# Five PSUM banks as five tiles in a spectral mixer with a gated feed-forward

## Chip, core and metric

One core of a Trainium2 chip. The metric is the time of one execution on the device in microseconds (us): 3697.88, the median of three runs (3697.82 to 3701.17).

## What is computed

For 8 sequences of 3072 positions and 256 channels: a real Fourier transform along the sequence, a complex 256x256 weight with a bias and a soft threshold on each frequency, the transform back; then for each of the 24576 rows an RMS norm and a gated feed-forward of width 1536.

```python
X = np.fft.rfft(x, axis=1); Xr, Xi = X.real, X.imag
Yr = Xr @ w_r - Xi @ w_i + b_r
Yi = Xr @ w_i + Xi @ w_r + b_i
Yr = np.sign(Yr) * np.maximum(np.abs(Yr) - 0.01, 0.0)      # Yi likewise
x = np.fft.irfft(Yr + 1j * Yi, n=3072, axis=1).reshape(24576, 256)
xn = x / np.sqrt(np.mean(x * x, axis=-1, keepdims=True) + 1e-06) * rms_g
g, val = xn @ w_gate, xn @ w_val
out = g * (1.0 / (1.0 + np.exp(-g))) * val @ w_out
```

## The kernel before

**The feed-forward.** The rows are cut into 48 tiles of 512, six to a sequence. A tile is transposed so that the channels lie on the partitions. The width of 1536 is cut into 12 slices of 128; a tile and a slice make a *step* (`step`, L944), 576 in all. A step multiplies its slice of the gate and value weights with the tile (the way up), takes Silu of the gate times the value (`h`), splits the product in a rounded half and a rest (`hs`, L952 and L953), and multiplies these with the slice of `w_out` into `acc` (the way down, `down`, L958 to L960), which is stored after twelve steps. Each fp32 product is three fp32r matmuls (high by high, high by low, low by high): this is why matmuls come in triples.

**Two ways up.** In 10 of the 48 tiles a step is *straight* (`straight`, L892): two sums of six 512-column matmuls into a g bank and a v bank (L901), Silu (L912), product (L913). In the other 38 tiles, 456 steps, it is *mixed* (`products`, L915): seven products of 128x128 by 256 columns in place of eight, from seven combinations `x` of the tile's blocks (`combine`) and weight combinations that are loaded for each step as `tr`. Product `own(0)` goes into `top` and is copied by ACT into `low` (L933), so that further products add to it there; ACT saves the pair of `add_` and `low` as it stands in `pq` (L935), more products add to both; DVE adds `pq` to the pair (`y`, L938); the last products go in, and ACT takes Silu of the pair of `top` and `low` (L941); DVE multiplies by `y` (L942). `top` and `add_` are halves of the g bank, `low` half of the v bank. So the pairs that L935, L938 and L941 read lie in two banks.

**The banks.** [...] One tile `up` (L288) holds five of them, `[P, 10, 256]`: halves 0 to 5 are three g banks, 6 to 9 two v banks; class `Bank` (L356) hands them out in turn. `acc` and `f` (the spectral products `pf`, `pm`, `pb` and transposes) have tiles of their own.

**The spectral work.** While a sequence's 72 steps run, the next sequence is transformed (`spectrum`): butterflies over 24 slots on DVE, then twelve units, each a forward product on PE (`pf`, L530), split, weight product (`pm`, L588 to L599), threshold, product back (`pb`, L650 to L658); butterflies and the norm at the end. During the last sequence's steps there is none of it.

**The order.** Every instruction group is first recorded by `op` with a due time in steps (`at`), an engine or two to choose from, a cost in us and the tokens that it reads and writes. `Plan.ordered` gives out buffers in turn; `Plan.schedule` places the groups one after the other on the engine that is free first, PE by smallest due time among what is ready; `emit` writes the program in this order, and the tile framework adds the semaphore waits, tile by tile. The plan counts each bank by itself (`BANKS`, L136). Constants set the due times: `LATER` for the way down, `DECODE` for the decoding of weights in the first sequence, `FIRST` and `LATER_ON` for the three parts of the spectral work within 72 steps, to which `BACK` is added.

```python
up_banks = pu.tile([P, 10, 256], F32, name="up")                                 # L288
pair = lambda k: up_banks[:, gb.h + k:vb.h + 1:vb.h - gb.h - k]                   # L921
```

## Time and profile before

| what | value |
|---|---|
| median of three runs | 3697.88 us |
| the profiled execution | 3696.22 us, span 3694.5 us |
| PE busy, its weight loads busy | 3098.2 us, 2771.7 us |
| DVE busy, ACT busy | 2259.1 us, 1879.8 us |
| mean granted TensorE clock | 0.994 |
| DMA | 577.69 MB, mean 156 GB/s |

The span runs from the first to the last instruction of the profiled execution. PE is TensorE's matmuls (their ends are modelled), PEld its weight loads, which one sequencer issues in front of them; DVE is VectorE, ACT is ScalarE, SP and POOL issue the DMAs. In a row, "up<-xn,tr" is written tile and read tiles, "idle before" the engine's idle time just in front of the group's instructions, and the names behind the arrows are the instructions whose end released them.

### The profile page before, as it was taken

The numbers are of one execution on the slowest core, as the hardware profiler recorded it, in microseconds if no ns is written. First come the engines' busy times: TensorE is split into PE (matmuls) and PEld (weight loads), VectorE is DVE, ScalarE is ACT, GpSimd is POOL, SyncE is SP. The second block draws the span as 40 slices with busy tenths as digits, with TensorE's granted clock in tenths as the row PEclk, the third lists the DMA queues.
The fourth block names the chain that finished last, engine by engine and source line by source line (L and its number), as shares of the span: only waits on it lengthen the run. The fifth ranks groups of instructions, "written<-read, shape, count | busy, mean of one in ns | idle before, by whom it ended". The sixth has DMA issues, their size and how long they took to land.

```text
span 3694.5 us, 56853 instructions
## 1 busy us (share of the span) xinstructions
PE 3098.2 (84%) x22147; PEld 2771.7 (75%) x22147; DVE 2259.1 (61%) x3994; ACT 1879.8 (51%) x3823; POOL 90.1 (2%) x176
## 2 busy tenths in 40 slices
PE   7679888889878888798888888888888888877777
PEld 6557876788768887787777887778877888766666
DVE  7786667656756557565675656756667566633343
ACT  2444655556545555455554555545554555443443
POOL 0000000000000000000000000000000000000000
PEclk9999999999999999999999999999999999999999
DMA  5354553455435554455544555345553555334443
GB/s 178 110 177 166 191 186 114 160 167 187 158 123 176 173 171 142 135 185 168 170 138 152 180 163 185 121 154 177 174 173 117 167 167 168 128 115 139 146 136 115
DMA packets 247023, 577.69 MB, mean 156 GB/s; under 512 B 23393, under 2 KB 80098, under 8 KB 246754
## 3 DMA queue, kind: packets, MB, share of 16 engines
q1 hardware_dynamic: 222562, 485.97, 39.7%
q0 software_dynamic: 24192, 88.09, 8.0%
q8 instruction: 174, 2.85, 0.3%
q14 instruction: 95, 0.78, 0.1%
HBM read 534.65 MB, written 39.32 MB: 155 GB/s over the span
## 4 chain that ended last, share of the span: by engine, by line
PE 71%; ACT 15%; DVE 10%; issue 3%; DVEq 0%; DMA 0%; ACTq 0%; SPq 0%
PE up L927 37%; PE acc L960 13%; PE up L901 10%; DVE y L938 6%; ACT pq L935 5%; ACT h L941 5%; ACT up L933 3%; PE pm L592 3%; PE pf L530 2%; DVE h L913 1%; ACT h L912 1%; PE up L710 1%; PE pm L588 1%; PE pb L655 1%; PE pt L867 1%
## 5 line engine op out<-in xcount | busy, mean ns | idle before, releaser
L927 PE MATMUL up<-xn,tr 128*128 128x256 f32 x5472 | 985.3, 293 | 262.6 <-ACT pq L935 86.8
L927 PEld LDWEIGHTS up<-xn,tr 128*128 128x128 f32 x5472 | 753.3, 188 | 395.1 <-ACT pq L935 124.3
L960 PE MATMUL acc<-wo,hs 128*128 128x256 f32 x6912 | 962.0, 279 | 2.2 <-DVE wo L810 1.1
L927 PE MATMUL up<-xn,wb 128*128 128x256 f32 x4104 | 730.8, 290 | 201.6 <-ACT h L941 94.2
L960 PEld LDWEIGHTS acc<-wo,hs 128*128 128x128 f32 x6912 | 874.4, 189 | 7.2 <-DVE wo L810 1.9
L927 PEld LDWEIGHTS up<-xn,wb 128*128 128x128 f32 x4104 | 569.4, 189 | 276.6 <-ACT h L941 123.6
L942 DVE TENSOR_TENSOR h<-h,y 128x512 f32<-128x512 f32 x456 | 315.2, 691 | 510.3 <-ACT h L941 509.0
L938 DVE TENSOR_TENSOR y<-up,pq 128x512 f32<-128x512 f32 x456 | 315.2, 691 | 405.6 <-PE up L927 304.3
L941 ACT ACTIVATE h<-up 128x512 f32<-128x512 f32 x456 | 272.4, 597 | 446.8 <-PE up L927 427.9
L935 ACT ACTIVATE pq<-up 128x512 f32<-128x512 f32 x456 | 272.4, 597 | 445.1 <-PE up L927 316.3
L953 DVE TENSOR_TENSOR hs<-h,hs 128x512 fp32r<-128x512 f32 x576 | 393.0, 685 | 100.4 <-ACT hs L952 99.2
L952 ACT ACTIVATE hs<-h 128x512 fp32r<-128x512 f32 x576 | 360.3, 626 | 88.6 <-PE acc L960 33.7
L901 PE MATMUL up<-xn,wb 128*128 128x512 f32 x1080 | 317.0, 404 | 43.2 <-ACT h L912 25.6
L933 ACT ACTIVATE up<-up 128x256 f32<-128x256 f32 x456 | 168.0, 368 | 345.5 <-PE up L927 245.8
L901 PEld LDWEIGHTS up<-xn,wb 128*128 128x128 f32 x1080 | 196.9, 190 | 106.8 <-ACT h L912 40.4
L912 ACT ACTIVATE h<-up 128x512 f32<-128x512 f32 x120 | 71.5, 596 | 192.5 <-PE up L901 169.7
L503 POOL DMA_DIRECT2D tab<-in_tabs_dram x168 | 89.3, 532 | 3047.1 <-PE pf L530 1491.0
L913 DVE TENSOR_TENSOR h<-h,up 128x512 f32<-128x512 f32 x120 | 81.3, 685 | 130.5 <-PE up L901 79.3
L901 PE MATMUL up<-xn,tb 128*128 128x512 f32 x360 | 128.5, 411 | 33.2 <-DVE h L913 23.6
L530 PE MATMUL pf<-tab,as 128*128 128x256 f32 x1008 | 134.0, 277 | 0.0
L530 PEld LDWEIGHTS pf<-tab,as 128*128 128x128 f32 x1008 | 123.9, 188 | 0.2
L592 PE MATMUL pm<-wm,xs 128*128 128x256 f32 x924 | 120.8, 277 | 0.0
(157 smaller groups left out, 3101.3 us busy)
## 6 DMA issues: line engine op xcount, KB each, us to landing
tr<-dt SPq DMA_DIRECT2D x456, 512.0 KB, 3.4
wo<-do SPq DMA_DIRECT2D x564, 256.0 KB, 2.7
tab<-in_tabs_dram POOLq DMA_DIRECT2D x168, 512.0 KB, 3.9
out_dram<-o SPq DMA_DIRECT2D x32, 512.0 KB, 3.2
seq<-in_x_dram SPq DMA_DIRECT2D x28, 512.0 KB, 5.4
tb<-db SPq DMA_DIRECT2D x27, 512.0 KB, 3.6
seq<-in_x_dram SPq DMA_DIRECT2D x25, 256.0 KB, 5.7
unit<-in_units_dram SPq DMA_DIRECT2D x12, 512.0 KB, 4.4
```

What stands on the lines that cost most here:

```text
L530: PE.matmul(ps[:, h, :], lhsT=r()[:, lp, ri, h * P:(h + 1) * P], rhs=f[:, rp, ri, :], start=(k + ri == 0), stop=(k == 2 and ri == 1),)
L592: PE.matmul(pm()[:, k], lhsT=(xr, xi)[k](lp, h), rhs=wm[:, rp, h, 1 + k, :], start=False, stop=(n == 2 and h == 1), skip_group_check=True,)
L901: PE.matmul((g, v)[k].flat(), lhsT=w(k, lp, c), rhs=xn()[:, rp, 2 * c:2 * c + 2, :].rearrange("p a b -> p (a b)"), start=((lp, rp, c) == t ...
L927: PE.matmul(dst(), lhsT=w(lp), rhs=xn()[:, rp, x, :], start=start and k == 0, stop=k == 2, skip_group_check=True)
L933: op("A", act(256), lambda _: A.activation(low(), top(), AF.Copy), [g], vb.first)
L935: op("A", act(512), lambda _: A.activation(pq()[:, ::-1, :], pair(1), AF.Copy), [g, v], pq.first)
L938: op("V", dve(512), lambda _: V.tensor_tensor(y(), pair(1), pq(), ALU.add), [g, v, pq.tok], y.first)
L941: op("A", act(512), lambda _: A.activation(s().rearrange("p (a b) -> p a b", a=2), pair(0), AF.Silu), [g, v], s.first)
L942: op("V", dve(512), lambda _: V.tensor_tensor(s(), s(), y().rearrange("p a b -> p (a b)"), ALU.mult), [y.tok], [s.tok])
L952: op("A", act(512), lambda _: A.activation(h()[:, 0], s(), AF.Copy), [s.tok], h.first)
L953: add(512, lambda f: f(h()[:, 1], s(), f32(h()[:, 0]), ALU.subtract), [s.tok], [h.tok])
L960: PE.matmul(o()[:, c, :], lhsT=h()[:, lp, c * P:(c + 1) * P], rhs=wo_()[:, rp, :], start=(i == 0 and k == 0 and c % 2 == 0), stop=(i == NF ...
```

## The change

The tile `up` becomes two pools of tiles of one bank each: two g banks and three v banks. `products` is rewritten so that each instruction of ACT and DVE works within one bank: `own(0)` and `mix(0)` go into the g bank (`p1`, `p5_`); ACT copies `p1` into `left` in the v bank (L931), ACT or DVE copies `p5_` into SBUF as `p5` (L932, 256 columns); after one product ACT copies `left` into `right` in the same bank (L934); after two more DVE adds `p5` to both halves (`y`, L938); Silu is done in two halves of 256, one from each bank (L939, L941). The 21 matmuls of a mixed step stay (L925 in place of L927), and so does the rest of the program. In the plan, `LATER` goes from 4.2 to 4.4, and the offsets of decoding and of the spectral work shift.

```diff
--- before.py
+++ after.py
@@ -32,12 +32,12 @@
 ORDER = [0, 9, 6, 3, 8, 4, 10, 2, 1, 7, 5, 11]
 LAM = 0.01
 PLAIN_OF = (5,)
-LATER = 4.2
+LATER = 4.4
 AHEAD = 60
-DECODE = (-4.5, -3.7, 0.4)
-BACK = 4.5
-FIRST = (16, 27, 50, 69.0)
-LATER_ON = (-1.5, 9, 48, 68)
+DECODE = (-5.0, -4.7, 0.4)
+BACK = 2.5
+FIRST = (16, 24.0, 51.5, 75.0)
+LATER_ON = (-3.0, 9, 48, 66.5)
 PLAIN = 3
 
 
@@ -133,7 +133,7 @@
 
     LAG = {"S": 2.2, "G": 3.0}
     STAY = 0.4
-    BANKS = ("gb0", "gb1", "gb2", "vb0", "vb1", "acc0", "f0")
+    BANKS = ("gb0", "gb1", "vb0", "vb1", "vb2", "acc0", "f0")
 
     def __init__(self):
         self.ops = []
@@ -271,7 +271,8 @@
 
     cp, bp, w1, w2, w4 = sbuf("cp", 1), sbuf("bp", 2), sbuf("w1", 1), sbuf("w2", 2), sbuf("w4", 4)
     wp, cq, q4, q3, q1, q2, sp = sbuf("wp", 1), sbuf("cq", 1), sbuf("q4", 4), sbuf("q3", 3), sbuf("q1", 1), sbuf("q2", 2), sbuf("sp", 1)
-    pu = ctx.enter_context(tc.tile_pool(name="pu", bufs=1, space=bass.MemoryType.PSUM))
+    pu = ctx.enter_context(tc.tile_pool(name="pu", bufs=2, space=bass.MemoryType.PSUM))
+    pv = ctx.enter_context(tc.tile_pool(name="pv", bufs=3, space=bass.MemoryType.PSUM))
     pa = ctx.enter_context(tc.tile_pool(name="pa", bufs=1, space=bass.MemoryType.PSUM))
     pf = ctx.enter_context(tc.tile_pool(name="pf", bufs=1, space=bass.MemoryType.PSUM))
     dp = ctx.enter_context(tc.tile_pool(name="dp", bufs=1, space=bass.MemoryType.DRAM))
@@ -285,7 +286,6 @@
     wb = cq.tile([P, NF, 3, 2, P], F32R, name="wb")
     dw = [[dp.tile([P, 2, n], F32, name=f"d{c}{i}") for i in range(NF)] for c, n in (("t", 512), ("o", D), ("b", 512))]
     df = [dp.tile([P, 2, 2, 2 * P], F32, name=f"df{g}") for g in range(NF // 2)]
-    up_banks = pu.tile([P, 10, 256], F32, name="up")
     ident = sp.tile([P, P], F32, name="ident")
     bias = sp.tile([P, 2, D], F32, name="bias")
     bias0 = sp.tile([P, D], F32, name="bias0")
@@ -327,7 +327,7 @@
         "seq": (bp, 2), "F": (w1, 1), "t4": (w1, 1), "o": (w1, 1), "m": (w1, 1), "a": (w1, 1), "k": (w1, 1), "z": (w1, 1),
         "ss": (w1, 1), "xf": (w1, 1), "xn": (w2, 2), "h": (w2, 2), "wo": (w4, 4),
         "tr": (q4, 4), "hs": (q3, 3), "G": (q1, 1), "as": (q1, 1), "xs": (q1, 1), "t3": (q1, 1), "st": (q1, 1), "pq": (q1, 1),
-        "gb": (None, 3), "vb": (None, 2), "acc": (pa, 1), "f": (pf, 1),
+        "gb": (pu, 2), "vb": (pv, 3), "acc": (pa, 1), "f": (pf, 1),
     }
 
     class Room:
@@ -357,11 +357,11 @@
 
 
         def __init__(self, tag, name):
-            super().__init__(tag, (), name)
-            self.h = 2 * (self.k % self.n) + (0 if tag == "gb" else 6)
+            super().__init__(tag, (P, 2, 256), name)
 
         def __call__(self, k=None):
-            return up_banks[:, self.h:self.h + 2] if k is None else up_banks[:, self.h + k]
+            t = super().__call__()
+            return t if k is None else t[:, k]
 
         def flat(self):
             return self().rearrange("p a b -> p (a b)")
@@ -913,13 +913,11 @@
         op("V", dve(512), lambda _: V.tensor_tensor(s(), s(), v.flat(), ALU.mult), [v.tok], [s.tok])
 
     def products(n, xn, i, s, tr):
-        pq, y = Room("pq", (P, 2, 256), f"pq{n}"), Room("m", (P, 2, 256), f"y{n}")
+        p5, y = Room("pq", (P, 256), f"p5{n}"), Room("m", (P, 2, 256), f"y{n}")
         own = lambda b: (lambda lp: wb[:, i, b, lp, :])
         mix = lambda b: (lambda lp: tr()[:, lp, P * b:P * (b + 1)])
-        gb, vb = Bank("gb", f"g{n}"), Bank("vb", f"v{n}")
-        g, v = gb.tok, vb.tok
-        top, low, add_ = (lambda: gb(0)), (lambda: vb(0)), (lambda: gb(1))
-        pair = lambda k: up_banks[:, gb.h + k:vb.h + 1:vb.h - gb.h - k]
+        one, two = Bank("gb", f"g{n}"), Bank("vb", f"v{n}")
+        p1, p5_, left, right = (lambda: one(0)), (lambda: one(1)), (lambda: two(0)), (lambda: two(1))
 
         def up(dst, w, x, tok, start=False):
             def go(_):
@@ -928,18 +926,20 @@
 
             op("P", mms(3, 256), go, [xn.part(f"h{k}") for k in (0, 2, 4, 6)] + [f"wb.{i // 2}", tr.tok], tok)
 
-        up(top, own(0), 0, gb.first + [f"go{n}"], True)
-        up(add_, mix(0), 4, [g])
-        op("A", act(256), lambda _: A.activation(low(), top(), AF.Copy), [g], vb.first)
-        up(low, mix(1), 5, [v])
-        op("A", act(512), lambda _: A.activation(pq()[:, ::-1, :], pair(1), AF.Copy), [g, v], pq.first)
-        up(low, mix(2), 1, [v])
-        up(add_, own(2), 6, [g])
-        op("V", dve(512), lambda _: V.tensor_tensor(y(), pair(1), pq(), ALU.add), [g, v, pq.tok], y.first)
-        up(low, mix(3), 3, [v])
-        up(top, own(1), 2, [g])
-        op("A", act(512), lambda _: A.activation(s().rearrange("p (a b) -> p a b", a=2), pair(0), AF.Silu), [g, v], s.first)
-        op("V", dve(512), lambda _: V.tensor_tensor(s(), s(), y().rearrange("p a b -> p (a b)"), ALU.mult), [y.tok], [s.tok])
+        up(p1, own(0), 0, one.first + [f"go{n}"], True)
+        up(p5_, mix(0), 4, [one.tok])
+        op("A", act(256), lambda _: A.activation(left(), p1(), AF.Copy), [one.tok], two.first)
+        op("AV", {"A": act(256), "V": dve(256)}, lambda e: A.activation(p5(), p5_(), AF.Copy) if e == "A" else V.tensor_copy(p5(), p5_()), [one.tok], p5.first)
+        up(left, mix(1), 5, [two.tok])
+        op("A", act(256), lambda _: A.activation(right(), left(), AF.Copy), [], [two.tok])
+        up(right, mix(2), 1, [two.tok])
+        up(left, own(2), 6, [two.tok])
+        up(p1, own(1), 2, [one.tok])
+        op("V", dve(512), lambda _: V.tensor_tensor(y(), two(), p5().unsqueeze(1).to_broadcast([P, 2, 256]), ALU.add), [two.tok, p5.tok], y.first)
+        op("A", act(256), lambda _: A.activation(s()[:, :256], p1(), AF.Silu), [one.tok], s.first)
+        up(right, mix(3), 3, [two.tok])
+        op("A", act(256), lambda _: A.activation(s()[:, 256:], right(), AF.Silu), [two.tok], [s.part("b")])
+        op("V", dve(512), lambda _: V.tensor_tensor(s(), s(), y().rearrange("p a b -> p (a b)"), ALU.mult), [y.tok, s.part("b")], [s.tok])
 
     def step(n, xn, i, mixed):
         s, h = Room("h", (P, 512), f"h{n}"), Room("hs", (P, 2, 512), f"hs{n}", F32R)
```

**PE, two mixed steps in the middle of the run.** Before, steps 312 to 314 of PE: `tr312` marks products of step 312 with loaded weights, `wb` those with resident ones; the fourth row's `tr313` belongs to step 313.

```order
L927 MATMUL up_147<-xn26_20353,wb_104 128x256 [waits Activation_49]
L927 MATMUL up_147<-xn26_20353,wb_104 128x256 x2
L960 MATMUL acc300_19823<-wo309_20217,hs309_20291 128x256 x3
L927 MATMUL up_147<-xn26_20353,tr313_20256 128x256 x3
L927 MATMUL up_147<-xn26_20353,wb_104 128x256 x3
L927 MATMUL up_147<-xn26_20353,tr314_20326 128x256 [waits DMAHW4_49]
L927 MATMUL up_147<-xn26_20353,tr314_20326 128x256 x2
L592 MATMUL pm5_3_20451<-wm_103,xs5_3_20384 128x256 [waits DVE_49]
L592 MATMUL pm5_3_20451<-wm_103,xs5_3_20384 128x256 x11
L927 MATMUL up_147<-xn26_20353,tr312_20198 128x256 [waits Activation_49]
L927 MATMUL up_147<-xn26_20353,tr312_20198 128x256 x2
```

The first row adds `own(2)` to step 312's g bank and waits for ACT; the row before the last adds to step 312's v bank and waits for ACT; all go to one tile, `up_147`. Now the same engine in steps 313 to 315 of the changed program, where `g314` and `v314` are the banks of step 314:

```order
L960 MATMUL acc300_20931<-wo310_21453,hs310_21536 128x256 [waits DMAHW3_49]
L960 MATMUL acc300_20931<-wo310_21453,hs310_21536 128x256 x2
L925 MATMUL v314_21683<-xn26_21465,tr314_21498 128x256 [waits Activation_49]
L925 MATMUL v314_21683<-xn26_21465,tr314_21498 128x256 x2
L960 MATMUL acc300_20931<-wo310_21453,hs310_21536 128x256 x6
L925 MATMUL v313_21619<-xn26_21465,tr313_21429 128x256 [waits DVE_49]
L925 MATMUL v313_21619<-xn26_21465,tr313_21429 128x256 x2
L925 MATMUL v314_21683<-xn26_21465,tr314_21498 128x256 [waits Activation_49]
L925 MATMUL v314_21683<-xn26_21465,tr314_21498 128x256 x2
L925 MATMUL v314_21683<-xn26_21465,wb_107 128x256 x3
L925 MATMUL g314_21666<-xn26_21465,wb_107 128x256 [waits Activation_49]
L925 MATMUL g314_21666<-xn26_21465,wb_107 128x256 x2
```

Step 314's triples now stand between those of step 313, each into a bank tile of its own step, and the waits for ACT and DVE stand in front of the triples that follow a copy or a sum in the same bank.

**ACT at the same place.** Before, with `pq312` and `pq313` the saved pairs of steps 312 and 313; the L933 between them is the copy of step 313:

```order
L935 ACTIVATE pq312_20448<-up_147 128x2x256 [waits PE_49]
L952 ACTIVATE hs311_20458<-h311_20400 128x512 [waits DVE_49]
L933 ACTIVATE up_147<-up_147 128x256 [waits PE_49,Activation_49]
L935 ACTIVATE pq313_20493<-up_147 128x2x256 [waits DVE_49]
L616 ACTIVATE t35_3_20504<-pm5_3_20451,lam_153 128x512 [waits PE_49]
L617 ACTIVATE k5_3_20512<-pm5_3_20451,lam_153 128x512
L941 ACTIVATE h312_20522<-up_147 128x512 [waits PE_49]
L933 ACTIVATE up_147<-up_147 128x256 [waits Activation_49]
```

Every L933, L935 and L941 here reads the one tile `up_147`, with the steps mixed. In the changed program, from the copy of step 314 on:

```order
L931 ACTIVATE v314_21683<-g314_21666 128x256 [waits PE_49]
L952 ACTIVATE hs312_21694<-h312_21646 128x512 [waits DVE_49]
L939 ACTIVATE h313_21701<-g313_21598 128x256 [waits PE_49]
L934 ACTIVATE v314_21683<-v314_21683 128x256 [waits PE_49]
L932 ACTIVATE p5314_21714<-g314_21666 128x256 [waits DVE_49]
L941 ACTIVATE h313_21701<-v313_21619 128x256 [waits PE_49]
L939 ACTIVATE h314_21732<-g314_21666 128x256 [waits DVE_49,PE_49]
L952 ACTIVATE hs313_21741<-h313_21701 128x512 [waits DVE_49,PE_49]
```

Here L931 and L934 are the copies into `v314`, L932 saves `p5` of step 314 behind a wait for DVE, and the Silu of a step is two rows, L939 and L941. Over the whole program `p5` falls to ACT in 250 steps and to DVE in 206. Of the triples that follow a reader in their own bank, 385 carry a wait for L931, 427 for L934 and 456 for L938.

## Rows read from the trace of the kernel before

**Rows 1.** The page: busy time by engine, and the chain's shares by engine.
```profile
PE 3098.2 (84%) x22147; PEld 2771.7 (75%) x22147; DVE 2259.1 (61%) x3994; ACT 1879.8 (51%) x3823; POOL 90.1 (2%) x176
...
PE 71%; ACT 15%; DVE 10%; issue 3%; DVEq 0%; DMA 0%; ACTq 0%; SPq 0%
```

**Rows 2.** Groups by line, PE's weight loads: busy, mean ns, idle before, releasers.
```profile
L927 PEld LDWEIGHTS up<-xn,tr 128*128 128x128 f32 x5472 | 753.3, 188 | 395.1 <-ACT pq L935 124.3 <-DVE y L938 118.0 <-ACT h L941 87.1
...
L927 PEld LDWEIGHTS up<-xn,wb 128*128 128x128 f32 x4104 | 569.4, 189 | 276.6 <-ACT h L941 123.6 <-ACT pq L935 81.0 <-ACT up L933 41.3
...
L901 PEld LDWEIGHTS up<-xn,wb 128*128 128x128 f32 x1080 | 196.9, 190 | 106.8 <-ACT h L912 40.4 <-DVE h L913 21.2 <-issue 2.5
...
L901 PEld LDWEIGHTS up<-xn,tb 128*128 128x128 f32 x360 | 64.9, 191 | 60.7 <-DVE h L913 35.8 <-ACT h L912 12.7
...
L592 PEld LDWEIGHTS pm<-wm,xs 128*128 128x128 f32 x924 | 112.6, 188 | 0.2 <-DVE pm L599 0.2
...
L655 PEld LDWEIGHTS pb<-ss,tab 128*128 128x128 f32 x462 | 59.3, 189 | 1.4 <-ACT pb L658 1.4
```

**Rows 3.** Timeline, 2071.9 to 2079.9 us: start, length, engine, instruction.
```profile
2072.81 0.37 ACT L933 ACTIVATE up<-up 128x256 f32<-128x256 f32 x1 [0.45 <-PE up L927]
2073.22 0.41 PEld L927 LDWEIGHTS up<-xn,wb 128*128 128x128 f32 x3 [0.72 <-ACT up L933]
...
2074.71 0.50 PE L927 MATMUL up<-xn,tr 128*128 128x256 f32 x3
...
2075.05 1.52 PE L592 MATMUL pm<-wm,xs 128*128 128x256 f32 x12
2075.32 0.69 DVE L938 TENSOR_TENSOR y<-up,pq 128x512 f32<-128x512 f32 x1 [1.56 <-PE up L927]
2076.05 0.60 ACT L935 ACTIVATE pq<-up 128x512 f32<-128x512 f32 x1 [2.87 <-DVE y L938]
...
2076.70 0.41 PEld L927 LDWEIGHTS up<-xn,tr 128*128 128x128 f32 x3 [0.32 <-ACT pq L935]
...
2077.84 0.50 PE L927 MATMUL up<-xn,wb 128*128 128x256 f32 x3
...
2078.18 0.50 PE L960 MATMUL acc<-wo,hs 128*128 128x256 f32 x3
2078.39 0.60 ACT L941 ACTIVATE h<-up 128x512 f32<-128x512 f32 x1 [0.50 <-PE up L927]
...
2078.53 1.52 PE L530 MATMUL pf<-tab,as 128*128 128x256 f32 x12
```

**Rows 4.** Groups by line, ACT and DVE: columns as in rows 2.
```profile
L938 DVE TENSOR_TENSOR y<-up,pq 128x512 f32<-128x512 f32 x456 | 315.2, 691 | 405.6 <-PE up L927 304.3 <-ACT up L933 70.6 <-PE up L901 12.0
...
L941 ACT ACTIVATE h<-up 128x512 f32<-128x512 f32 x456 | 272.4, 597 | 446.8 <-PE up L927 427.9 <-PE up L901 14.8 <-DVE seq L451 3.2
...
L935 ACT ACTIVATE pq<-up 128x512 f32<-128x512 f32 x456 | 272.4, 597 | 445.1 <-PE up L927 316.3 <-DVE y L938 128.5
...
L933 ACT ACTIVATE up<-up 128x256 f32<-128x256 f32 x456 | 168.0, 368 | 345.5 <-PE up L927 245.8 <-DVE y L938 91.2 <-DVE h L913 4.0
...
L599 DVE TENSOR_TENSOR pm<-pm,bias 128x256 f32<-128x256 f32 x154 | 66.0, 429 | 69.7 <-PE pm L588 68.7
```

**Rows 5.** Windows: start:end, length, busy PE, PEld, DVE, ACT, POOL, clock, DMA share, GB/s.
```profile
134.00:585.00 451.00, 383.27 (x2427) 327.76 (x2425) 319.45 (x599) 239.98 (x504) 13.27 (x25) 0.98 0.52 171
1028.00:1475.00 447.00, 383.10 (x2796) 347.05 (x2797) 279.57 (x487) 238.64 (x488) 12.73 (x24) 0.99 0.50 160
3252.00:3695.00 443.00, 340.54 (x2464) 299.37 (x2464) 163.64 (x258) 174.65 (x333) 0.00 (x0) 1.00 0.40 133
```

**Rows 6.** DMA issues, the row of `tr`: count, KB each, us to landing.
```profile
tr<-dt SPq DMA_DIRECT2D x456, 512.0 KB, 3.4
```

**Rows 7.** Windows of ten us before and at the first step, columns as rows 5.
```profile
120.00:130.00 10.00, 1.04 (x5) 0.57 (x3) 9.62 (x24) 6.08 (x16) 0.00 (x0) 0.78 0.14 52
130.00:140.00 10.00, 6.91 (x25) 5.04 (x26) 7.29 (x20) 4.63 (x9) 0.00 (x0) 0.70 0.62 190
```

## The prediction

> **What bounds the kernel now.** I read the page's shares first, then the groups of instructions, then the timeline of eight microseconds, then the work of three stretches. The shares [rows 1] say PE 84%, DVE 61%, ACT 51%; ends of matmuls are modelled, so for PE I take its weight loads, busy 2771.7 of 3694.5 us. PE's loads are idle for 922.8 us, and the chain that ended last gives ACT and DVE together 25% of the span: PE is the engine with most to do, but it is stopped again and again. The groups say where [rows 2]: before the loads of matmuls into `up` PE is idle 395.1 + 276.6 (mixed steps) + 106.8 + 60.7 (straight steps) = 839.2 us, nearly all of the 922.8, and the releasers are ACT's copies and Silu and DVE's sum, the readers of `up`.
>
> The timeline [rows 3] shows why. At 2072.81 ACT copies (L933); at 2073.22 PE starts a group that had to wait 0.72 us for it. By the order in the section on the change, that group is the product `own(2)` of step 312 and the copy is step 313's: they share no bank, only the tile `up`. The same at 2076.05 and 2076.70: ACT saves step 313's pair (L935), and a later product of step 312 waits for it. In this stretch no matmul into `up` runs while ACT or DVE reads `up`, and the readers themselves start only when the `up` matmuls issued ahead of them have ended. Matmuls into other tiles do run beside such readers: 12 into `pm` from 2075.05 while DVE (L938) and ACT (L935) read `up`, taking 1.52 us, as the 12 at 2078.53 do; the readers keep 0.69 and 0.60 us, their means over the whole run [rows 4]. So banks can be used side by side, and what is ordered is the tile.
>
> **The change, part by part.** *Five tiles.* A matmul now waits only for readers of its own bank's tile. In the new order step 313's and 314's triples wait for instructions of their own step. This takes away all of the idle time above: -839.2 us, to 2855.3. It can be a little more: a stop also leaves a load's end uncovered (a triple's loads take 0.41 to 0.43 us, back to back a triple comes every 0.34), about 0.08 us at each stop.
>
> *Waits that remain.* A mixed step has three places where PE needs a result from its own bank: after the copy to `left`, after the copy to `right`, after the sum `y`; 456 x 3 = 1368. What one needs: from the end of a triple's slot to the reader's start 0.21 us on ACT (2077.84 plus 0.34 to 2078.39) and 0.27 on DVE (2074.71 plus 0.34 to 2075.32), the reader (0.37 for a copy of 256, 0.69 for the sum, [rows 4]), and 0.04 to 0.05 until the next load (2076.65 to 2076.70): 0.63 us after a copy, 1.01 after the sum. What covers it: matmuls that stand between in PE's new order, 0.114 us each. Counted over the program, 9 or more (1.03 us) stand there in 378 of the 385 first waits, in 424 of the 427 second ones and in all 456 third ones; the median third has 12 (1.37 us). So an undelayed reader is just in time nearly everywhere, and PE pays only where a reader is late because its engine was busy. That has no row of its own. From below: the same pattern inside one bank exists in the spectral work, 77 copies in `pb` that cost PE 1.4 us together and 154 sums in `pm` that cost 0.2 [rows 2], at most 0.02 us each: 27 us. From above: what today's waits cost, 671.7 us for the four readers of each of 456 mixed steps, 0.37 each: 506 us. I take 0.05 us, near the lower row, because the cover is planned there in the same way, but above it because the third wait has little to spare and both engines will be fuller: 1368 x 0.05 = 68 us.
>
> *ACT and DVE.* Gone per mixed step: L935 and L941 (0.597 each). Added on ACT: one more copy of 256 and two Silu of 256, and `p5` in 250 of the 456 steps, at 0.368 each (L933): 456 x 3 x 0.368 + 250 x 0.368 - 544.8 = +51 us. On DVE `p5` in 206 steps, at 0.429 (L599, 256 out of PSUM): +88 us. The sum with `p5` broadcast keeps 0.691; no row has a broadcast operand, so between 0.69 and twice a 256 (0.86). Beside a span of 2924 this makes ACT 66% and DVE 80%. I cost it at nothing: PE's matmuls hide it. If that cover goes, it is the second rival. [...]
>
> *Two g banks and three v banks.* A straight step takes one of each, so two are in flight, as before. In a mixed step the g bank is given back after the first Silu, earlier than the v bank. Only 70 of the 456 starts of a mixed step carry a wait for the Silu of two steps before; I add nothing beyond the 68 us.
>
> *Offsets of the plan.* No instruction is added; the spectral chain and the weight decoding come 0.5 to 2 steps earlier, down products 0.2 later. Each has one answer, 0 us, as long as DVE holds both streams. In the stretch 1028 to 1475 its 279.6 us plus a seventh of 88 stand beside 347.1 us of PE's loads; in 134 to 585 319.5 stand beside 327.8 [rows 5], the tightest place. SP's loads: between the matmul that frees a buffer of `tr` and the first that reads its next content stand at least 55 matmuls (6.3 us), against 3.4 us to landing [rows 6]: free, though steps come faster.
>
> **Sum.** 3694.5 - 839.2 + 68 = 2923 us of span; the profiled execution took 1.7 us more than its span, and the median of the runs is another 1.7 above that: 2926 us. The last eighth shows the same from another side: without spectral work (3252 to 3695) it lasts as long as the others, 443 us, with PE's loads busy 299 [rows 5]; it should fall to about 310.
>
> **The rivals.** *DVE sets the pace in mixed steps.* Each step's `y` and product wait in DVE's queue behind spectral sums, and `y(n)` also needs the product of step n-1, since `y` and `p5` have one buffer each. If one instruction of 512 (0.60 us) per mixed step comes on top of the cover, 456 x 0.6 = 274 us: 3198 us. For it: 80% busy, and the little to spare behind `y`. Against it: in the last eighth, where DVE is at 37%, it can't hold. Chance 0.10.
>
> *Slower: the steps go one at a time.* ACT's queue is in order. Where `p5` falls to ACT it waits for `y` of the step before, and the next copies and Silu stand behind it. If by this no cover holds, PE stands 0.63 + 0.63 + 1.01 = 2.27 us in each mixed step: 456 x 2.27 = 1035 us, 3890 plus 3, that is 3893 us. It is slower than now from 842 us on, when four fifths of these needs lie bare. Against it: in the new order the neighbour steps and `acc` stand between each pair. Chance 0.01.
>
> *Slower by the clock.* [...] Chance 0.01.
>
> *The order stays.* If tiles of the pools were still ordered against each other, nothing would move: 3698 us. The new order's waits inside a step speak against it. Chance 0.02.
>
> **How the numbers follow.** My case has 0.86. Its own ends: 2815, when nothing comes back and half of the uncovered load ends go too (-40, 0.08 us at 500 stops); 3115, when a wait costs 0.19 us, half of today's 0.37 (+260). I give those ends 0.78 of the 0.86; up to 3140 some of the DVE rival comes in, which makes 0.80. About 0.2% is what a measurement of this kernel can tell from no change; my case and the DVE rival are both faster by more: faster 0.96, same 0.02, slower 0.02.
>
> **What would show it.** Right: PE's loads idle before the up matmuls fall from 839 to under 110 us, and up matmuls run while ACT or DVE read another step's bank; PE's loads are busy over 90% of the span; DVE near 80%, ACT near 66%; the last eighth near 310 us. The DVE rival: the third wait (after `y`) carries most of the idle time, and DVE is idle little before L938 and L942. The first slower rival: idle time before both copies' triples, 0.6 us each. [...] I am wrong if the idle time before the up matmuls stays above 260 us, or if the time comes back where no up matmul waits.

## The result and the profile after

The changed kernel takes 2839.28 us (median of four runs, 2838.38 to 2840.0) against 3697.85 us for the kernel before: a ratio of 0.7676, 95% interval 0.7663 to 0.769. The forecast was 2926 us with a range from 2815 to 3140: the direction and the range held, and the time came out 87 us under the forecast.

The page of the changed kernel: busy time by engine, then the shares by engine of the chain that ended last (span 2838.0 us, before 3694.5).

```profile
PE 2787.4 (98%) x22147; PEld 2702.2 (95%) x22147; DVE 2297.4 (81%) x4211; ACT 1906.8 (67%) x4518; POOL 90.4 (3%) x176
...
PE 96%; DVE 3%; DMA 0%; ACT 0%; issue 0%; SPq 0%; ACTq 0%; DVEq 0%
```

Against [rows 1] the number of matmuls is the same, and so is the work; PE has filled up. ACT and DVE, a quarter of the chain before, have all but left it (DVE 3%). DVE and ACT are at the shares that were forecast, 80% and 66%.

PE's weight loads by line, columns as in [rows 2]:

```profile
L960 PEld LDWEIGHTS acc<-wo,hs 128*128 128x128 f32 x6912 | 888.9, 189 | 19.8 <-ACT sq L751 9.1 <-DMA wo<-do 1.3 <-DVE hs L953 1.0
L925 PEld LDWEIGHTS v<-xn,tr 128*128 128x128 f32 x4104 | 567.6, 188 | 2.4 <-ACT v L934 0.7
L925 PEld LDWEIGHTS g<-xn,wb 128*128 128x128 f32 x2736 | 378.9, 188 | 0.0
L925 PEld LDWEIGHTS g<-xn,tr 128*128 128x128 f32 x1368 | 191.4, 188 | 0.0
L925 PEld LDWEIGHTS v<-xn,wb 128*128 128x128 f32 x1368 | 191.4, 188 | 0.0
...
L901 PEld LDWEIGHTS g<-xn,wb 128*128 128x128 f32 x720 | 129.9, 190 | 26.6 <-DVE wb L810 0.8 <-ACT wb L809 0.7 <-ACT h L912 0.6
L901 PEld LDWEIGHTS v<-xn,wb 128*128 128x128 f32 x360 | 68.2, 189 | 16.6
L901 PEld LDWEIGHTS v<-xn,tb 128*128 128x128 f32 x360 | 66.2, 190 | 15.4 <-DVE tb L810 1.0 <-ACT tb L809 0.4 <-DVE h L913 0.3
```

In mixed steps the idle time before the up loads was 395.1 + 276.6 us [rows 2]; it is 2.4 us for the 9576 matmuls of L925. In straight steps it was 167.5 us and is 58.6, and the rows name a releaser for about 4 us of these. The view names releasers only for gaps over 0.15 us, and the rest is shorter gaps; the first point of the section on the prediction says what they are.

The timeline of the changed kernel from 1562.28 to 1564.86 us, steps 298 and 299, columns as in [rows 3]:

```profile
1562.28 0.50 PE L925 MATMUL v<-xn,tr 128*128 128x256 f32 x3
...
1562.62 0.50 PE L925 MATMUL v<-xn,wb 128*128 128x256 f32 x3
1562.76 0.38 ACT L934 ACTIVATE v<-v 128x256 f32<-128x256 f32 x1
...
1562.96 0.84 PE L960 MATMUL acc<-wo,hs 128*128 128x256 f32 x6
1563.16 0.69 DVE L938 TENSOR_TENSOR y<-v,p 128x512 f32<-128x512 f32 x1
...
1563.64 0.50 PE L925 MATMUL v<-xn,tr 128*128 128x256 f32 x3
...
1563.95 0.39 ACT L932 ACTIVATE p<-g 128x256 f32<-128x256 f32 x1 [0.81 <-DVE y L938]
1563.98 0.50 PE L925 MATMUL v<-xn,wb 128*128 128x256 f32 x3
...
1564.32 0.50 PE L925 MATMUL v<-xn,tr 128*128 128x256 f32 x3
...
1564.86 0.38 ACT L941 ACTIVATE h<-v 128x256 f32<-128x256 f32 x1 [0.53 <-PE v L925]
```

By the program's order the copy at 1562.76 belongs to step 299, while the triples at 1562.28 and 1562.62 add to the v bank of step 298. At 1563.16 DVE sums step 298's v bank (L938, until 1563.85), and at 1563.64 PE adds to that of step 299: matmuls into one v bank run beside a reader of another. This is so over the whole run: counted in the trace, an up matmul starts while a reader of the way up (L931 to L941, L912, L913) runs in 1924 of 2976 cases; in the kernel before it did so in none of 2064. The triple that needs step 298's sum is issued at 1564.32, 0.47 us after the sum ended. In its place PE did 12 other matmuls from 1562.96 on. The waits now lie where they cost nothing: ACT waits 0.81 us for the sum before it may overwrite `p5` (L932), and 0.53 us for PE before the Silu at 1564.86.

ACT's and DVE's groups on the way up, which answer to [rows 4]:

```profile
L938 DVE TENSOR_TENSOR y<-v,p 128x512 f32<-128x512 f32 x456 | 314.0, 689 | 174.1 <-PE v L925 165.8 <-ACT h L939 2.8
...
L939 ACT ACTIVATE h<-g 128x256 f32<-128x256 f32 x456 | 174.4, 382 | 68.5 <-PE g L925 62.7 <-ACT o L974 0.5 <-ACT seq L772 0.3
L941 ACT ACTIVATE h<-v 128x256 f32<-128x256 f32 x456 | 174.0, 382 | 98.1 <-PE v L925 93.0
L931 ACT ACTIVATE v<-g 128x256 f32<-128x256 f32 x456 | 169.7, 372 | 73.2 <-PE g L925 69.6
L934 ACT ACTIVATE v<-v 128x256 f32<-128x256 f32 x456 | 169.7, 372 | 92.7 <-PE v L925 90.5
...
L932 ACT ACTIVATE p<-g 128x256 f32<-128x256 f32 x250 | 95.6, 383 | 27.3 <-DVE y L938 24.7
L932 DVE COPY p<-g 128x256 f32<-128x256 f32 x206 | 86.7, 421 | 16.6 <-ACT v L931 13.2
```

Now ACT and DVE wait for PE. By these groups ACT does 783.4 us where L933, L935 and L941 were 712.8 us [rows 4]: +71, with +51 forecast, since a Silu of 256 takes 0.382 us, the save 0.383 and the copies 0.372, where the forecast has 0.368 for all. DVE gained 86.7 - 1.2 = 85.5 us, with 88 forecast. The sum with the broadcast `p5` keeps its 0.69 us.

Two windows of the changed kernel, columns as in [rows 5]: the sixth tile of the third sequence, which is straight (the butterflies of the next sequence lie there), and the last sequence, without spectral work.

```profile
1123.50:1176.00 52.50, 52.50 (x313) 45.98 (x312) 48.59 (x93) 35.82 (x94) 0.00 (x0) 1.00 0.54 168
...
2546.60:2838.00 291.40, 286.31 (x2467) 286.11 (x2465) 172.50 (x285) 186.46 (x451) 0.00 (x0) 1.00 0.65 204
```

The last sequence took 443 us with 299 us of loads [rows 5]; it takes 291, with 286 us of loads, and the clock is 1.00. The time before the first step was shorter too: the first matmul of the way up starts at 114.0 us, before at 134.5. So of the 856.5 us the start gave 20.5, the stretch between 3117.5 - 2432.6 = 684.9, and the last sequence (from 3252.0 and from 2546.6 on) 442.5 - 291.4 = 151.1.

### The profile page after: what moved, and what is told of

Read it like the earlier page. It is cut to its first block, busy times and chain, and to the rows that moved or that the text cites. A ratio compares the mean times of both kernels' runs of the same rounds, so it can differ in the third digit from the quotient of the medians.

```text
span 2838.0 us, 57978 instructions
## 1 busy us (share of the span) xinstructions
PE 2787.4 (98%) x22147; PEld 2702.2 (95%) x22147; DVE 2297.4 (81%) x4211; ACT 1906.8 (67%) x4518; POOL 90.4 (3%) x176
## 4 chain that ended last, share of the span: by engine, by line
PE 96%; DVE 3%; DMA 0%; ACT 0%; issue 0%; SPq 0%; ACTq 0%; DVEq 0%
PE acc L960 28%; PE v L925 22%; PE g L925 17%; PE v L901 6%; PE g L901 6%; PE pf L530 4%; PE pm L592 4%; PE pm L588 2%; PE pb L655 2%; PE pt L867 2%; PE pb L650 1%; PE pm L710 1%; PE pm L570 1%; PE pb L729 1%; PE pf L688 0%; PE pb L633 0%
## 5 line engine op out<-in xcount | busy, mean ns | idle before, releaser
L960 PE MATMUL acc<-wo,hs 128*128 128x256 f32 x6912 | 986.8, 279 | 11.0 <-ACT sq L751 9.0
L960 PEld LDWEIGHTS acc<-wo,hs 128*128 128x128 f32 x6912 | 888.9, 189 | 19.8 <-ACT sq L751 9.1
L925 PE MATMUL v<-xn,tr 128*128 128x256 f32 x4104 | 682.3, 280 | 0.5 <-ACT v L934 0.5
L925 PEld LDWEIGHTS v<-xn,tr 128*128 128x128 f32 x4104 | 567.6, 188 | 2.4 <-ACT v L934 0.7
L953 DVE TENSOR_TENSOR hs<-h,hs 128x512 fp32r<-128x512 f32 x576 | 395.2, 686 | 83.3 <-ACT hs L952 83.2
L925 PE MATMUL g<-xn,wb 128*128 128x256 f32 x2736 | 457.9, 279 | 0.0
L938 DVE TENSOR_TENSOR y<-v,p 128x512 f32<-128x512 f32 x456 | 314.0, 689 | 174.1 <-PE v L925 165.8
L925 PEld LDWEIGHTS g<-xn,wb 128*128 128x128 f32 x2736 | 378.9, 188 | 0.0
L941 ACT ACTIVATE h<-v 128x256 f32<-128x256 f32 x456 | 174.0, 382 | 98.1 <-PE v L925 93.0
L925 PE MATMUL g<-xn,tr 128*128 128x256 f32 x1368 | 232.4, 279 | 0.0
L925 PE MATMUL v<-xn,wb 128*128 128x256 f32 x1368 | 232.3, 278 | 0.0
L934 ACT ACTIVATE v<-v 128x256 f32<-128x256 f32 x456 | 169.7, 372 | 92.7 <-PE v L925 90.5
L939 ACT ACTIVATE h<-g 128x256 f32<-128x256 f32 x456 | 174.4, 382 | 68.5 <-PE g L925 62.7
L931 ACT ACTIVATE v<-g 128x256 f32<-128x256 f32 x456 | 169.7, 372 | 73.2 <-PE g L925 69.6
L901 PE MATMUL g<-xn,wb 128*128 128x512 f32 x720 | 190.8, 400 | 1.2 <-DVE wb L810 0.5
L925 PEld LDWEIGHTS g<-xn,tr 128*128 128x128 f32 x1368 | 191.4, 188 | 0.0
L925 PEld LDWEIGHTS v<-xn,wb 128*128 128x128 f32 x1368 | 191.4, 188 | 0.0
L901 PEld LDWEIGHTS g<-xn,wb 128*128 128x128 f32 x720 | 129.9, 190 | 26.6 <-DVE wb L810 0.8
```

Of the source, the lines that this page charges most:

```text
L901: PE.matmul((g, v)[k].flat(), lhsT=w(k, lp, c), rhs=xn()[:, rp, 2 * c:2 * c + 2, :].rearrange("p a b -> p (a b)"), start=((lp, rp, c) == t ...
L925: PE.matmul(dst(), lhsT=w(lp), rhs=xn()[:, rp, x, :], start=start and k == 0, stop=k == 2, skip_group_check=True)
L931: op("A", act(256), lambda _: A.activation(left(), p1(), AF.Copy), [one.tok], two.first)
L934: op("A", act(256), lambda _: A.activation(right(), left(), AF.Copy), [], [two.tok])
L938: op("V", dve(512), lambda _: V.tensor_tensor(y(), two(), p5().unsqueeze(1).to_broadcast([P, 2, 256]), ALU.add), [two.tok, p5.tok], y.first)
L939: op("A", act(256), lambda _: A.activation(s()[:, :256], p1(), AF.Silu), [one.tok], s.first)
```

## The experiments

Each kernel was timed beside the kernel before, whose median was 3697.55 us for the first four runs, 3698.23 for the next four and 3699.14 for the last two. My theory was that the one tile orders all its readers and writers, and that five tiles are the whole gain. Against it stood the new arrangement within a bank, the new offsets, and, for what is left, DVE.

| run | edit | us | ratio to before (95%) |
|---|---|---|---|
| e1_one_tile | changed kernel, banks in one tile | 3995.35 | 1.0807 (1.0786 to 1.0829) |
| e2_split_pairs | old arrangement, five tiles | 2844.72 | 0.7695 (0.7684 to 0.7706) |
| e3_old_offsets | changed kernel, old offsets | 2838.38 | 0.7675 (0.7662 to 0.7687) |
| e4_new_offsets | kernel before, new offsets | 3694.89 | 0.9993 (0.9983 to 1.0003) |
| e5_banks32 | three g banks, two v banks | 2840.58 | 0.7679 (0.7663 to 0.7695) |
| e6_dve_load | one more DVE operation a step | 2908.7 | 0.7862 (0.7849 to 0.7876) |
| e7_no_lag | plan without its cross-engine allowance | 2997.1 | 0.8101 (0.8086 to 0.8115) |
| e8_all_mixed | sixth tiles mixed too | 2867.92 | 0.7753 (0.7738 to 0.7767) |
| e9_mixed_p5_act | e8, `p5` always on ACT | 2883.08 | 0.7794 (0.778 to 0.7807) |
| e10_p5_act | changed kernel, `p5` always on ACT | 2839.23 | 0.7672 (0.7661 to 0.7684) |

### The new arrangement in one tile

```diff
-    pu = ctx.enter_context(tc.tile_pool(name="pu", bufs=2, space=bass.MemoryType.PSUM))
-    pv = ctx.enter_context(tc.tile_pool(name="pv", bufs=3, space=bass.MemoryType.PSUM))
+    pu = ctx.enter_context(tc.tile_pool(name="pu", bufs=1, space=bass.MemoryType.PSUM))
+    up_banks = pu.tile([P, 10, 256], F32, name="up")
-            return t if k is None else t[:, k]
+            return up_banks[:, self.h:self.h + 2] if k is None else up_banks[:, self.h + k]
```

> The changed kernel with its five banks put back into one tile; the new products, the two g and three v banks and the plan's offsets stay. Theory A, waits are ordered by the tile: each access of ACT and DVE lies within one bank here, and the order of the tile comes back all the same. In the built order 9 matmuls no longer stand behind most readers (median 0 to 4 for L938, L939, L941, L931, L934), so PE stops as before: loads idle before the up matmuls 750 to 900 us, time 3600 to 3750 us. Rival B, accesses that span two banks were what had to wait, or the new arrangement of the products is what gained: 2830 to 2950 us, idle time under 100 us.

Measured: 3995.35 us, 8% slower than the kernel before. It is on theory A's side, but I had the size wrong: I looked for about the time of before, and for at most 900 us of idle time before the up matmuls, which is 1072.7 with the 189.1 of the straight steps. Its weight loads in mixed steps:

```profile
L925 PEld LDWEIGHTS up<-xn,tr 128*128 128x128 f32 x5472 | 753.5, 190 | 547.8 <-DVE y L938 125.8 <-ACT p L932 114.0 <-ACT h L939 96.9
L925 PEld LDWEIGHTS up<-xn,wb 128*128 128x128 f32 x4104 | 565.0, 190 | 335.8 <-ACT h L941 114.8 <-ACT h L939 73.9 <-DVE y L938 60.2
```

No sum, save or Silu reads two banks here, and still each reader stops PE. (Only L931 touches two, since it copies from the g bank to the v bank as L933 did; "each instruction of ACT and DVE works within one bank", in the section on the change, goes too far there.) Counted in the trace, no up matmul starts beside any of the 2976 readers. The idle time is 883.6 us against 671.7 [rows 2]: there are six readers in a mixed step (L931, L932, L934, L938, L939, L941) where there were four, so 883.6 / 2736 = 0.32 us a reader, and 0.37 before. So work within one bank alone buys nothing, and the new arrangement, with its order, costs 298 us as long as the tile is one. A part of these is the clock: its mean is 0.985 here and 0.994 in the kernel before, and 0.009 of 3995 us makes about 36 us, an estimate.

### The old arrangement in five tiles

```diff
-        op("A", act(512), lambda _: A.activation(pq()[:, ::-1, :], pair(1), AF.Copy), [g, v], pq.first)
+        def save(_):
+            A.activation(pq()[:, 1], add_(), AF.Copy)
+            A.activation(pq()[:, 0], low(), AF.Copy)
+        op("A", 2 * act(256), save, [g, v], pq.first)
...
```

The sum and the Silu are split into two instructions in the same way; the five banks are three g tiles and two v tiles; the offsets are those of before.

> The kernel before with five tiles of one bank each (three g, two v) and nothing else new: its products, its offsets; the three instructions that took a pair from two banks (L935, L938, L941) become two instructions each, one for each bank. Theory A: the tiles alone give nearly all: 2830 to 2920 us, PE's loads idle before the up matmuls under 100 us, though ACT and DVE get 3 x 456 more instructions (ACT about 70% busy, DVE about 84%). Rival B, the new arrangement of copies and Silu is needed too: over 3050 us.

Measured: 2844.72 us, that is 853 of the 858 us. Its page, and the group of up matmuls in mixed steps that waits longest (L938 is the matmul here, L929 the sum):

```profile
PE 2787.8 (98%) x22147; PEld 2695.6 (95%) x22147; DVE 2245.8 (79%) x4441; ACT 1924.7 (68%) x4744; POOL 90.2 (3%) x176
...
L938 PEld LDWEIGHTS v<-xn,tr 128*128 128x128 f32 x4104 | 571.1, 188 | 9.5 <-DVE y L929 7.6 <-ACT v L944 0.2
```

The tiles are the gain, once no instruction takes a pair across two of them; the new arrangement adds 5 or 6 us at most (2839.28, or 2838.38 with the offsets of before). Its first step starts at 112.9 us, and that of the changed kernel with old offsets at 113.8, while the one-tile runs start at 133.9 (e1) and 135.6 (e4): the 20 us at the start come from the tiles too. The first units (`unit_start`, L672) take their banks from the same tile.

### The offsets, and how the banks are shared out

```diff
-LATER = 4.4
+LATER = 4.2
...
```

> The changed kernel with the plan's offsets of the kernel before (way down, decoding, spectral work). Theory A, the offsets cost and give next to nothing once no wait is left: 2825 to 2870 us. Rival C, the offsets are what brought the time below the forecast of 2926: 2880 to 2960 us, with stops of PE at the turn of the sequences or in the first one.

> The kernel before with the new offsets of the plan alone. Theory A: 3670 to 3730 us, with 800 to 860 us of idle time before the up matmuls. Rival C, the offsets have a share of the gain of their own: under 3620 us.

Measured: 2838.38 us (2834.81 to 2844.13) with the old offsets in the changed kernel, 3694.89 us with the new ones in the kernel before. In the second, PE's loads are idle 813.7 us before the up matmuls. Neither time can be told from its parent's; the offsets are worth nothing in either kernel.

```diff
-        "gb": (pu, 2), "vb": (pv, 3), "acc": (pa, 1), "f": (pf, 1),
+        "gb": (pu, 3), "vb": (pv, 2), "acc": (pa, 1), "f": (pf, 1),
```

> The changed kernel with three g banks and two v banks, as the kernel before had them, in place of two and three. Theory A, no bank is waited for: 2830 to 2860 us. Rival, the third v bank is what lets two mixed steps overlap: over 2900 us, with PE stopped before the triples that follow the first copy.

Measured: 2840.58 us. Two and three or three and two makes no difference here.

### More work for DVE

```diff
-        add(512, lambda f: f(h()[:, 1], s(), f32(h()[:, 0]), ALU.subtract), [s.tok], [h.tok])
+        for _ in range(2):
+            add(512, lambda f: f(h()[:, 1], s(), f32(h()[:, 0]), ALU.subtract), [s.tok], [h.tok])
```

> The changed kernel with DVE's subtraction for the rest half of hs (L953) done twice in every step, with the same result: 576 more instructions of 512, 0.60 us each back to back, 346 us more for DVE, the plan knows their cost. DVE goes from 81% to about 92% of the span. Theory A, PE's matmuls hide it as long as DVE is not full: 2840 to 2920 us. The DVE rival of the prediction, DVE's queue is on the path of the sum y: near 2839 + 346 = 3185 us, with idle time of PE after the sum (before the triples that follow L938).

Measured: 2908.7 us. DVE's busy time rose by 300 us and the span by 69 (lines from L953 on are one higher):

```profile
PE 2810.2 (97%) x22147; PEld 2712.4 (93%) x22147; DVE 2597.1 (89%) x4728; ACT 1927.7 (66%) x4577; POOL 90.2 (3%) x176
...
L961 PEld LDWEIGHTS acc<-wo,hs 128*128 128x128 f32 x6912 | 893.6, 189 | 53.1 <-DVE hs L954 30.2 <-ACT o L975 12.2 <-DVE wo L810 1.5
L925 PEld LDWEIGHTS v<-xn,tr 128*128 128x128 f32 x4104 | 560.3, 189 | 10.6 <-ACT v L934 6.6 <-DVE y L938 1.2 <-ACT v L931 0.7
```

The 300 us are less than the 346 expected: the plan has two engines to choose from for some groups, and it put 41 saves of `p5` (L932) and 18 scalings of the norm (L774 and L772) on ACT that DVE had before. PE waits for the doubled operation itself, on the way down (30.2 us), and hardly for the sum `y` (1.2). Over the whole run DVE at 81% isn't the bound: three quarters of its added time is hidden.

### The plan's allowance

`Plan.schedule` counts a result as ready for another engine 0.18 us after its planned end (0.06 us on ACT and DVE themselves). Without that allowance a matmul may be placed closer behind the reader that it needs.

```diff
-self.LAG.get(e, 0.18 if far else 0.0 if e == "P" else 0.06)
+self.LAG.get(e, 0.0)
```

> The changed kernel with the plan's allowance for a signal between engines (0.18 us, and 0.06 on one engine) set to 0, so that the order leaves fewer matmuls behind each reader: 9 or more in 204 of 403 first waits, 182 of 450 second ones, 237 of 456 third ones, against nearly all. Theory A, the cover in PE's order is why the waits cost nothing: with 0.63 us needed after a copy and 1.01 after the sum the uncovered part adds up to 100 to 170 us, and late readers add some: 2940 to 3060 us, the idle time before the v triples. Rival D, the cover has little to do with it, and any order with separate tiles runs at PE's pace: 2835 to 2870 us.

Measured: 2997.1 us, 158 more than the changed kernel. Its loads with the longest wait:

```profile
L925 PEld LDWEIGHTS v<-xn,tr 128*128 128x128 f32 x4104 | 566.0, 188 | 84.7 <-DVE y L938 79.7
```

That PE doesn't wait inside a mixed step is the order's work: with the same five tiles and a tighter order the wait behind the sum comes back, 80 us, at the place with the least to spare. The other 78 us lie elsewhere: the loads are busy 38 us longer (2740.5), and PE's loads are idle some 36 us more before other groups, the transposes (L867) with 15 above all. 12 us of this fall before the first step, which starts at 126.4.

### The sixth tiles mixed too

```diff
-PLAIN_OF = (5,)
+PLAIN_OF = ()
```

> The changed kernel without the seven straight tiles after the first sequence's start (every sixth tile): all tiles but the first three are mixed, 84 steps more. If PE's own matmuls set the time now, as theory A has it, each such step saves three matmuls of 256 columns (12 of 512 count as 24, 21 of 256 in their place), 84 x 3 x 0.116 = 29 us: 2800 to 2820 us, though DVE gets 84 more sums (83% busy). If ACT or DVE or the loads set it, 2840 us or more.

Measured: 2867.92 us, 29 slower than the changed kernel where I had looked for a gain. A mixed step has 21 matmuls of 256 columns and a straight one 12 of 512, so PE, the bound, has less to do and the sum of the work says faster. The sixth tiles of the first and of the third sequence in this run, columns as in [rows 5] (the third's in the changed kernel stands above, 52.50 us):

```profile
441.90:499.20 57.30, 51.20 (x382) 48.93 (x381) 53.99 (x95) 41.90 (x124) 0.00 (x0) 0.91 0.66 218
...
1143.20:1198.70 55.50, 51.19 (x415) 48.92 (x414) 54.33 (x104) 45.93 (x137) 0.00 (x0) 1.00 0.65 216
```

In the third sequence DVE is busy 54.33 of 55.50 us, against 48.59 of 52.50 in the changed kernel: PE is busy less (51.19 for 52.50), and the tile takes 3.0 us longer. PE's loads aren't full either (48.92 us). In the first sequence it takes 57.3 us instead of 49.1, at a granted clock of 0.91. Taken from a tile's first up matmul to the next tile's, six of the seven sixth tiles are 5.6 to 7.4 us longer than in the changed kernel, with DVE busy 52.6 to 54.9 of 55.4 to 55.9 us (the tile behind four of them is 3.0 us shorter); in the seventh sequence DVE is busy 42.7 of 50.7 us and the loss is 0.9 us. So in these tiles DVE is full, as the rival "DVE sets the pace" had it for all. That DVE is what holds PE up there isn't shown by that: in the third sequence's tile PE's loads wait 3.6 us for DVE (2.8 of it for the sum) and 2.9 us for ACT. A part of the 29 us is the clock: its mean is 0.991 over this run and 0.994 in the changed kernel, and 0.003 of 2869 us makes about 9 us, an estimate. Whether relieving DVE gives the time back was the next question; the control is the same edit in the changed kernel:

```diff
-        op("AV", {"A": act(256), "V": dve(256)}, lambda e: A.activation(p5(), p5_(), AF.Copy) if e == "A" else V.tensor_copy(p5(), p5_()), [one.tok], p5.first)
+        op("A", act(256), lambda _: A.activation(p5(), p5_(), AF.Copy), [one.tok], p5.first)
```

> As the run in which the sixth tiles are mixed too, but the save of p5 goes to ACT in all 540 steps. That run took 2867.9 us; its sixth tiles take 55.5 us each, with DVE busy 54.3 of them and PE's loads 48.9. Theory A: in the sixth tile, where the butterflies lie, DVE sets the pace. Eight of the twelve saves stood on DVE there, 0.42 us each, so 3.4 us a tile go away, 7 x 3.4 = 24 us: 2840 to 2852, and DVE's busy time there falls to about 51 us. Theory B: the extra time comes from waits inside the mixed steps' chain (copy, save, Silu on ACT in order), so a p5 that waits for y of the step before now holds up ACT's queue in every step: 2868 to 2900.

> The changed kernel with the save of p5 on ACT in all 456 steps: 206 x 0.42 = 87 us less on DVE (78% instead of 81%), 206 x 0.38 = 79 us more on ACT (70%). Theory A: PE's matmuls cover both, and nothing moves: 2835 to 2845. Theory B: a p5 that waits in ACT's queue for y of the step before holds up the copies behind it, as in the slower rival of the prediction: over 2850, with idle time before the loads at L925 that ACT's copies release.

Measured: 2883.08 us for e9, 15 slower still, and 2839.23 us for e10, no change. The third sequence's sixth tile in e9, then three stretches inside it:

```profile
1142.30:1200.90 58.60, 53.24 (x413) 51.25 (x412) 56.40 (x104) 46.65 (x142) 0.00 (x0) 0.94 0.63 210
...
1158.50:1160.00 1.50, 0.11 (x1) 0.11 (x2) 1.50 (x3) 1.50 (x6) 0.00 (x0) 1.00 0.91 288
1160.00:1162.00 2.00, 2.00 (x10) 2.00 (x11) 1.97 (x4) 1.50 (x6) 0.00 (x0) 0.52 0.72 267
1162.00:1166.00 4.00, 4.00 (x31) 4.00 (x30) 3.37 (x5) 2.38 (x8) 0.00 (x0) 0.82 0.29 95
```

The timeline of e9 just before and in the first of these stretches:

```profile
1156.40 2.91 ACT L772 ACTIVATE seq<-seq,rs 128x256 f32<-128x256 f32 x7 [0.54 <-DVE rs L764]
...
1159.47 0.37 ACT L932 ACTIVATE p<-g 128x256 f32<-128x256 f32 x1
1159.89 0.59 PEld L925 LDWEIGHTS g<-xn,wb 128*128 128x128 f32 x3 [1.59 <-ACT p L932]
1159.89 0.89 PE L925 MATMUL g<-xn,wb 128*128 128x256 f32 x3 [1.40 <-ACT p L932]
```

Theory A falls in the form I gave it: DVE's busy time in the tile didn't drop (56.40 us), and the tile grew by 3.1 us. By the rows of the two windows the eight saves (3.4 us) did leave DVE, but six more operations of the butterflies (L420 to L436), two more sums and two more scalings lie in the window, which is 3.1 us longer. Butterflies and sums are as many as before over the run, so they only lie elsewhere in time; of the scalings the plan puts 70 on DVE (L774) instead of 52. The save of `p5` now stands in ACT's queue behind seven scalings of the norm (L772), and PE waits 1.59 us for it. That is the mechanism of theory B, but at this place with another instruction ahead of `p5` than I named: not the sum `y` but the norm. Over the run PE's loads wait 24.7 us for `p5` on ACT and 23.7 for the sum, where in e8 they wait 4.2 us for `p5` on DVE and 17.4 for the sum; the granted clock is 0.990. Whether a plan that knew of this would make the mixed sixth tiles pay, stays open. With the sixth tiles straight (e10) ACT can take all 456 saves at no cost.

None of these runs beats the changed kernel by more than the measurement tells apart; with PE at 98% little is left to beat.

## Why the prediction was right, point by point

**The idle time, -839.2.** The mechanism is shown: e1 and e2 separate the tile from the new arrangement. The size was wrong by 58.6 us, since I counted all idle time of the straight steps as waits. The sixth tile shows what it is: PE is busy for all of its 52.50 us and the loads for 45.98, so there are 6.52 us of gaps. 5.20 of them stand before the 144 loads of L901, 0.036 us each; over the 1440 straight matmuls that makes 52 of the 58.6 us. Where loads of L901 follow one another they take 0.188 us and start every 0.233, and the matmuls of 512 columns start every 0.233 too (medians): a load is shorter than the time from matmul to matmul, and the loads' idle time is not PE's. What was taken away is 839.2 - 61.0 = 778.2 us.

**The waits that remain, +68.** This term was mis-sized: 2.4 us instead of 68, or 0.002 us for each of the 1368 waits instead of 0.05. Even the lower bound, 0.02 from the spectral work, was too high. I moved away from it because both engines would be fuller and the third wait had little to spare; the cover of 12 matmuls held, and e7 shows that the third wait is the one to break first. The two errors nearly cancel, by luck: -778 us measured, -771 forecast.

**The load ends.** This is the step that missed the time. I named them (0.08 us at each stop), put 40 us of them into the range's lower end and nothing into the sum. The page's busy time of the loads fell from 2771.7 to 2702.2 us with the same 22147 loads at 188 ns: 69.5 us, or some 870 stops at 0.08. The trace bears it out: the lengths of all loads add up to 4221 us before and 4224 after, but neighbours overlap by 1529 us instead of 1459, and there are 53 gaps of more than 0.05 us between loads instead of 1204. It is 69.5 of the 85 us by which the span is under the forecast; 7 come from the point above and 9 from idle time elsewhere.

**The start, 0.** I hadn't looked for other users of the tile. The first units use it, and the first step starts 20.5 us sooner, with DVE busy 101 us ahead of it in both kernels. (These us are part of the idle time and load ends above.)

**ACT and DVE, 0 on the path.** Right, and tested: 67% and 81% for the forecast 66% and 80%; 300 us more on DVE cost 69 (e6), 206 more saves on ACT nothing (e10). This holds for the straight sixth tiles; mixed, they have no such room (e8). The halved Silu has a price on ACT: its two halves take 0.17 us more than the one of 512 (2 x 0.382 against 0.597). None of it shows in the time.

**Banks and offsets, 0.** Right (e3, e4, e5).

**The transfers.** Right: only 1.3 us of PE's idle time before L960 is put down to `wo`, and none to `tr`, though `tr` now lands in 3.9 us where it took 3.4 [rows 6]:

```profile
tr<-dt SPq DMA_DIRECT2D x456, 512.0 KB, 3.9
```

**The last eighth.** Forecast 310 us, measured 291. Of the 19 us the loads' ends are 13 (busy 299.4 before, 286.1 now), and the rest is waits that did not come.

**The rivals.** DVE as the pace of all mixed steps (3198): not so. In the sixth tiles, once they are mixed, DVE is full (e8), but taking the saves from it gave nothing back (e9), so even there the pace isn't shown to be DVE's alone. Steps one at a time (3893): the wait for the sum in front of `p5` exists, 24.7 us on ACT in all, and stops nobody. The order stays (3698): no.

The clock (chance 0.01): no. Its mean is 0.994 over the run as before; it falls to 0.50 in the first sequence, as before, for 6.8 to 13.7 us each at 104, 179 and 196 us, and from 203 us to the end it is 1.00. In the kernel before it still fell to 0.50, for 3.4 us each time, at 610, 1081, 1371 and 2703 us, behind stretches of 3.0 to 3.3 us in which PE was busy for 1.57 to 1.71 us. In that kernel matmuls of 256 columns start every 0.213 us while the clock is 0.50 and every 0.116 at 1.00 (medians). The first of these places, columns as in [rows 5]:

```profile
607.00:610.30 3.30, 1.63 (x10) 1.24 (x10) 2.53 (x6) 1.30 (x3) 0.00 (x0) 1.00 0.57 181
610.50:613.70 3.20, 2.68 (x13) 2.39 (x12) 1.02 (x2) 0.72 (x3) 0.00 (x0) 0.50 0.09 36
```

So the clock did fall behind stops inside the steps, two times in the stretch for which [rows 5] has 0.99. Counted from 260 us on, it fell 4 times before, 16 times in e1, which has the most idle time before the up matmuls (1072.7 us, mean clock 0.985), and not once in the changed kernel (61.0 us). In e9 it stayed at 1.00 through a stop of PE of 1.4 us that followed two shorter ones (0.17 and 0.43 us), and was 0.52 in the two us behind it; how long a stop must be for this, no run shows. The rival fails with its stops nearly gone, and with the stops of the kernel before the mean was 0.994 too.

## What to carry to other kernels

Make buffers that are meant to be used side by side separate objects for whatever inserts the waits: turning through banks inside one tile gave no overlap of readers and writers here (0 of 2976 readers in e1, 1924 of 2976 with five tiles), even where the sums, saves and Silus kept to one bank. When such a wait is taken away, look at what the order puts between a result and its use, for that decides whether the next wait shows (12 matmuls did, the tighter order of e7 did not), and add the ends of loads that each stop had left bare. Judge spare room by the stretch with the most work for the engine and not by its share of the run: DVE at 81% took 300 us more at a price of 69, while in the sixth tiles, with the mixed steps' work added, it was full.

## What the runs showed that I had not expected

- Finer instructions in one tile were a loss: 8% slower, with 0.32 us of stop for each of six readers, and a clock that fell 16 times (e1).
- Less work for the engine that is the bound made the kernel slower by 29 us (e8): the same edit added work to DVE in its fullest stretch, and the sixth tiles are where the time went. Which engine's queue holds PE up there stays open.
- The page's busy time of ACT rose by 27 us although its groups' sum rose by about 67: the page counts overlapping ends of neighbours once. The same holds for PE's loads, and is why the load ends show in the page's total and not in the groups (753.3 + 569.4 us before, 1329.3 after).
